# Evening out the slots of a fused FFT and GEGLU kernel, and two-pass values for five blocks in six

## The chip, the cores and the metric

The kernel runs on one core of a Trainium2 chip. The metric is device time in microseconds (us), the median of several runs. All runs quoted here are in the same (fast) state, with a granted TensorE clock of 0.994 to 1.0. PE is TensorE (PEld its weight loads), DVE is VectorE, ACT is ScalarE and POOL is GpSimd. PSUM is the memory that matmuls write to, in banks; copying a result out of a bank is called an *eviction* here.

## The reference, cut to what matters

```python
X = np.fft.fft(np.fft.fft(x, axis=1), axis=2).real      # x: 8 batches x 3008 x 256
g   = X @ w_gate                                        # 256 -> 1536
val = X @ w_val
out = (gelu(g) * val) @ w_out                           # 1536 -> 256
```

The kernel does the FFT as matmuls ("DFT work"). It uses the symmetry of a real input's transform: a token k and its mirror have the same even part E and odd part O, so gate and value are needed at E + O and at E − O.

## The kernel before

A batch has 3 chunks of 512, 512 and 481 token pairs, and a chunk has 12 blocks (`fc`) of 128 of the 1536 hidden columns. One turn of the loop over blocks is a *slot*. The weights "O" and "M" are the odd part and −2 times it, so a pass with M on top of E + O gives E − O in the same PSUM bank.

In the traces below, a matmul that starts a new result waits until the last reader of its bank is done. The kernel uses eight PSUM banks (2 + 3 + 1 + 2), and hands them out by tag:

```python
ps_g   bufs=2    # gate           ps_o   bufs=1    # layer-2 output
ps_v   bufs=3    # value          ps_dft bufs=2    # DFT
```

First half of a block, and second half (one slot later):

```python
def apart(ci, fc):
    return fc % 3 != 2 and (b, ci) != (0, 0)            # two blocks of three

def l1_first(ci, fc):
    pg = ps_g()
    mm(pg, "g", "E", E); mm(pg, "g", "O", O)            # (cut: slices, flags)
    activation(gl[:, 0], pg, Gelu)                      # ACT, first gelu
    pv = ps_v()
    if apart(ci, fc):                                   # value in two passes
        mm(pv, "v", "E", E)
        po = ps_v()
        mm(po, "v", "M", O)
        ve = EB * w128 + pv                             # DVE: three operations
        vv[:, 0]        = -0.5 * po + ve
        vv[:, reversed] =  0.5 * po + ve
    else:                                               # value in three passes
        mm(pv, "v", "E", E); mm(pv, "v", "O", O)
        h[:, fc, 0] = gl[:, 0] * pv                     # DVE

def l1_second(ci, fc):
    mm(pg, "g", "M", O)
    if apart(ci, fc):
        activation(gl[:, reversed], pg, Gelu)           # ACT, second gelu
        h[:, fc] = gl * vv                              # POOL, both halves
    else:
        mm(pv, "v", "M", O)
        activation(gl[:, 1], pg, Gelu)
        h[:, fc, reversed] = gl[:, 1] * pv              # DVE
```

Layer 2 of a chunk runs in the next chunk's slots, in 8 units of 12 matmuls each. *Filler* is DFT work of the next batch, spread over the slots. A slot was:

```python
for fc in range(NFC):                                   # NFC = 12
    first[fc]()
    ... DFT filler of the next batch ...
    if fc > 0: second[fc - 1]()
    tgt = len(pend) * (fc + 1) // NFC                   # 0 1 2 2 3 4 4 5 6 6 7 8
    while done < tgt: pend[done](); done += 1           # a unit: 12 matmuls
```

So two slots of three had 12 layer-2 matmuls and the third had none. The order in the program is not quite the order on the engine: the build moves some instructions ahead.

## Time and profile before

| | before |
|---|---|
| time | 719.29 us (median of 4 runs beside the changed kernel, 718.97 to 719.59) |
| busy: PE, DVE, ACT, POOL | 96%, 80%, 65%, 58% |
| value blocks in two / three passes | 184 / 104 |
| period of one batch in the steady state | 84.9 us |

These lines are from the page of the kernel before: the engines' busy time, the chain of waits by engine, and three groups of instructions (line, engine, operation, output and inputs, count, then busy us and mean ns of one, then the idle time of the engine before them and what ended most of it).

```profile
PE 688.0 (96%) x5274; PEld 460.5 (64%) x5336; DVE 572.3 (80%) x923; ACT 466.9 (65%) x892; POOL 412.2 (58%) x242
...
PE 88%; ACT 5%; DVE 4%; issue 2%; DMA 1%; POOL 0%; ACTq 0%; DVEq 0%
...
L551 POOL TENSOR_TENSOR h_sb<-gelu_sb,v_sb 128x1024 bf16<-128x1024 bf16 (+1 forms) x184 | 387.1, 2105 | 277.2 <-ACT gelu_sb L550 156.8
...
L524 DVE SCALAR_TENSOR_TENSOR ve_sb<-EB_sb,w_97,ps_v 128x512 f32<-128x512 bf16 (+1 forms) x184 | 134.1, 733 | 66.2 <-PE ps_v L502 66.0
...
L550 ACT ACTIVATE gelu_sb<-ps_g 128x512 bf16<-128x512 f32 (+1 forms) x184 | 108.6, 590 | 19.2 <-PE ps_g L502 17.7
```

PE is the engine to look at, but its busy share can't tell how much there is to gain. The Trainium skill says so in "Perfetto Trace Analysis", section "Identifying the Most-Contended Engine": matmul busy share is not a good measure of the distance from the roofline. What can be counted is the distance between the starts of two matmuls. For bf16 it is 216 ns for 512 columns, 203 for 481 and 109 for 256 when nothing is in the way. I call what a distance has beyond that a *gap*, and put it down to the PSUM tag that the late matmul writes.

The timeline of the kernel before, in a slot without layer 2, shows two such gaps. Its columns are start and duration in us, engine, line, operation, output and inputs, shapes and count.

```profile
325.84 0.38 PE L502 MATMUL ps_v<-EO_sb,WvE 128*128 128x512 bf16 x1
...
326.06 0.38 PE L502 MATMUL ps_v<-EO_sb,WvM 128*128 128x512 bf16 x1
...
326.26 0.75 DVE L524 SCALAR_TENSOR_TENSOR ve_sb<-EB_sb,w_97,ps_v 128x512 f32<-128x512 bf16 x1 [1.08 <-PE ps_v L502]
...
326.50 0.38 PE L502 MATMUL ps_g<-EO_sb,WgM 128*128 128x512 bf16 x1
...
326.72 0.38 PE L502 MATMUL ps_v<-EO_sb,WvM 128*128 128x512 bf16 x1
...
327.06 0.38 PE L502 MATMUL ps_v<-EO_sb,WvE 128*128 128x512 bf16 x1
...
327.20 0.59 ACT L554 ACTIVATE gelu_sb<-ps_g 128x512 bf16<-128x512 f32 x1
...
327.50 0.38 PE L502 MATMUL ps_g<-EO_sb,WgM 128*128 128x512 bf16 x1
...
327.84 0.38 PE L502 MATMUL ps_g<-EO_sb,WgE 128*128 128x512 bf16 x1
```

The value matmul at 327.06 comes 0.34 us after the matmul before it, not 0.216. It needs a value bank, and the DVE operation that reads one (326.26, 0.75 us long) ended at 327.01. The gate matmul at 327.84 again comes 0.34 us after its predecessor. The second gelu that frees a gate bank ran from 327.20 to 327.79.

### The profile page before, as it was taken

Reading aid. Unit: us, or ns where it says so; the run is one execution under the profiler, and the core shown is the slowest. Engines: PE = TensorE matmul, PEld = TensorE weight load, DVE = VectorE, ACT = ScalarE, POOL = GpSimd, SP = SyncE. Lnnn points to the kernel's source line nnn. Section 1 sums busy time; section 2 is a strip of 40 time slices with the busy share of each in tenths; the row PEclk is TensorE's granted clock in tenths of the full one; section 3 lists DMA queues with packets and bytes.
Section 4 is the critical chain, followed back from the end, with each engine's and each line's share of the span. In section 5 each row is a group of like instructions: output and inputs, shape, how many; then the busy total and the mean of one; then the engine's idle time right before and its main releaser. Section 6 shows DMA issues by size and latency. Waiting matters only on the chain.

```text
span 716.7 us, 14298 instructions
## 1 busy us (share of the span) xinstructions
PE 688.0 (96%) x5274; PEld 460.5 (64%) x5336; DVE 572.3 (80%) x923; ACT 466.9 (65%) x892; POOL 412.2 (58%) x242
## 2 busy tenths in 40 slices
PE   2899999999999999999999999999999999999995
PEld 2556666666667666666666666666666766666664
DVE  7698888798877888788877888779887788888870
ACT  6688567766676666766677656776668666666650
POOL 8205565655556565666566656555565656576760
PEclk9999999999999999999999999999999999999999
DMA  9951512431115111151212421111111111211122
GB/s 247 205 118 23 124 31 46 86 72 35 41 38 119 42 34 43 33 121 38 45 31 53 105 45 34 43 36 37 35 41 42 30 44 31 45 41 38 42 45 66
DMA packets 36277, 43.43 MB, mean 61 GB/s; under 512 B 6668, under 2 KB 33292, under 8 KB 34700
## 3 DMA queue, kind: packets, MB, share of 16 engines
q1 hardware_dynamic: 32432, 30.47, 17.8%
q0 software_dynamic: 3184, 11.57, 8.8%
q8 instruction: 41, 0.67, 0.4%
q10 hardware_dynamic: 592, 0.49, 0.3%
q14 instruction: 28, 0.23, 0.1%
HBM read 29.43 MB, written 24.64 MB: 75 GB/s over the span
## 4 chain that ended last, share of the span: by engine, by line
PE 88%; ACT 5%; DVE 4%; issue 2%; DMA 1%; POOL 0%; ACTq 0%; DVEq 0%
PE ps_o L573 33%; PE ps_g L502 23%; PE ps_v L502 20%; PE ps_dft L402 6%; PE ps_dft L365 3%; ACT gelu_sb L517 1%; ACT gelu_sb L554 1%; ACT A_sb L379 1%; PE ps_dft L427 1%; PE ps_dft L440 1%; DVE x_sb L236 1%; ACT out_sb L591 1%; DVE EO_sb L456 1%; PE ps_dft L452 1%; DVE h_sb L536 1%
## 5 line engine op out<-in xcount | busy, mean ns | idle before, releaser
L551 POOL TENSOR_TENSOR h_sb<-gelu_sb,v_sb 128x1024 bf16<-128x1024 bf16 (+1 forms) x184 | 387.1, 2105 | 277.2 <-ACT gelu_sb L550 156.8
L573 PE MATMUL ps_o<-Wo_sb,h_sb 128*128 128x256 bf16 (+1 forms) x2304 | 295.5, 272 | 4.0 <-DVE out_sb L584 2.2
L573 PEld LDWEIGHTS <-h_sb 128*128 128x128 bf16 (+1 forms) x2304 | 227.7, 100 | 68.3 <-issue 9.4
L517 ACT ACTIVATE gelu_sb<-ps_g 128x512 bf16<-128x512 f32 (+1 forms) x288 | 169.8, 590 | 123.2 <-PE ps_g L502 115.2
L524 DVE SCALAR_TENSOR_TENSOR ve_sb<-EB_sb,w_97,ps_v 128x512 f32<-128x512 bf16 (+1 forms) x184 | 134.1, 733 | 66.2 <-PE ps_v L502 66.0
L528 DVE SCALAR_TENSOR_TENSOR v_sb<-ps_v,ve_sb 128x512 f32<-128x512 f32 (+1 forms) x184 | 124.4, 676 | 13.9 <-POOL h_sb L551 0.5
L530 DVE SCALAR_TENSOR_TENSOR v_sb<-ps_v,ve_sb 128x512 f32<-128x512 f32 (+1 forms) x184 | 123.3, 670 | 0.0
L550 ACT ACTIVATE gelu_sb<-ps_g 128x512 bf16<-128x512 f32 (+1 forms) x184 | 108.6, 590 | 19.2 <-PE ps_g L502 17.7
L502 PE MATMUL ps_v<-EO_sb,WvE 128*128 128x512 bf16 (+1 forms) x288 | 107.8, 374 | 3.2
L502 PE MATMUL ps_g<-EO_sb,WgE 128*128 128x512 bf16 (+1 forms) x287 | 107.4, 374 | 1.6
L502 PE MATMUL ps_v<-EO_sb,WvM 128*128 128x512 bf16 (+1 forms) x288 | 108.0, 375 | 0.3 <-DVE v_sb L530 0.2
L502 PE MATMUL ps_g<-EO_sb,WgM 128*128 128x512 bf16 (+1 forms) x287 | 107.9, 376 | 0.1
L555 DVE TENSOR_TENSOR h_sb<-gelu_sb,ps_v 128x512 bf16<-128x512 bf16 (+1 forms) x104 | 69.7, 671 | 32.5 <-ACT gelu_sb L554 32.5
L591 ACT ACTIVATE out_sb<-ps_o 128x512 f32<-128x512 f32 x92 | 54.8, 595 | 51.2 <-PE ps_o L573 51.2
L502 PE MATMUL ps_g<-EO_sb,WgO 128*128 128x512 bf16 (+1 forms) x231 | 86.4, 374 | 0.0
L536 DVE TENSOR_TENSOR h_sb<-gelu_sb,ps_v 128x512 bf16<-128x512 bf16 (+1 forms) x104 | 69.9, 673 | 5.2 <-ACT gelu_sb L517 4.0
L554 ACT ACTIVATE gelu_sb<-ps_g 128x512 bf16<-128x512 f32 (+1 forms) x104 | 61.0, 590 | 6.3 <-PE ps_g L502 6.2
L412 DVE CAST Z_sb<-ps_dft 128x512 bf16<-128x512 f32 x88 | 60.1, 684 | 1.3 <-PE ps_dft L402 1.3
L402 PE MATMUL ps_dft<-CS,A_sb 128*128 128x256 bf16 x372 | 60.8, 274 | 0.4 <-DVE EO_sb L456 0.3
L402 PEld LDWEIGHTS <-A_sb 128*128 128x128 bf16 x384 | 37.8, 99 | 28.9 <-issue 1.8
L365 PEld LDWEIGHTS <-x_sb 94*128 94x128 bf16 x512 | 31.9, 102 | 31.3 <-DVE x_sb L236 14.9
L379 ACT ACTIVATE A_sb<-ps_dft 128x384 bf16<-128x384 f32 x115 | 50.9, 496 | 0.3 <-PE ps_dft L365 0.3
(102 smaller groups left out, 433.2 us busy)
## 6 DMA issues: line engine op xcount, KB each, us to landing
out_dram<-out_sb SPq DMA_DIRECT2D x361, 64.0 KB, 2.0
x_sb<-in_x_dram POOLq DMA_DIRECT2D x14, 752.0 KB, 8.1
x_plain<-in_x_dram SPq DMA_DIRECT2D x4, 384.0 KB, 7.6
x_plain<-in_x_dram SPq DMA_DIRECT2D x2, 768.0 KB, 7.6
Wo_sb<-in_moe_w_out_dram POOLq DMA_DIRECT2D x2, 384.0 KB, 5.8
wg_hi<-in_moe_w_gate_dram SPq DMA_DIRECT2D x2, 256.0 KB, 3.8
wv_hi<-in_moe_w_val_dram SPq DMA_DIRECT2D x2, 256.0 KB
wg_lo<-in_moe_w_gate_dram SPq DMA_DIRECT2D x2, 256.0 KB, 4.4
```

The costliest lines, as they stand in the source:

```text
L402: nc.tensor.matmul(ps[:, d * C : (d + 1) * C], A[:, cc, k2 + d, :], CS[:, cc, :], start=(cc == 0), stop=(cc == 1),)
L502: nc.tensor.matmul(ps[:, :n], W[nm, part][:, fs], src, start=start, stop=stop, **kw)
L517: nc.scalar.activation(gl[:, 0, :n], pg[:, :n], AF.Gelu)
L524: nc.vector.scalar_tensor_tensor(ve[:, :n], EB_bufs[b][:, c0 : c0 + n], w128[:, fc : fc + 1], pv[:, :n], op0=ALU.mult, op1=ALU.add)
L528: nc.vector.scalar_tensor_tensor(vv[:, 0, :n], po[:, :n], -0.5, ve[:, :n], op0=ALU.mult, op1=ALU.add)
L530: nc.vector.scalar_tensor_tensor(_sub(vv, [[-1, n]], TOK + n - 1), po[:, :n], 0.5, ve[:, :n], op0=ALU.mult, op1=ALU.add)
L536: nc.vector.tensor_tensor(st["h"][:, fc, 0, :n], gl[:, 0, :n], pv[:, :n], op=ALU.mult)
L550: nc.scalar.activation(_sub(gl, [[-1, n]], TOK + n - 1), pg[:, :n], AF.Gelu)
L551: nc.gpsimd.tensor_tensor(st["h"][:, fc, :, :n], gl[:, :, :n], pv[:, :, :n], op=ALU.mult)
L554: nc.scalar.activation(gl[:, 1, :n], pg[:, :n], AF.Gelu)
L555: nc.vector.tensor_tensor(_sub(st["h"], [[-1, n]], (fc * 2 + 1) * TOK + n - 1), gl[:, 1, :n], pv[:, :n], op=ALU.mult)
L573: nc.tensor.matmul(pso[:m, sign, :], st["h"][:, fc, sign, h0 : h0 + m], Wo_sb[:, fc, :], start=(fc == 0), stop=(fc == NFC - 1),)
```

## The change

Its intent: spread the work that DVE, ACT and POOL must do behind PE evenly over the slots, so that more blocks can use the two-pass value, which has one matmul less. Layer 2 comes in pieces of 4 matmuls, two per slot. The second gate pass moves from behind the filler to right behind the next block's first gate pass. Five blocks of six are in two passes.

```diff
         def apart(ci, fc):
-            return fc % 3 != 2 and (b, ci) != (0, 0)
+            return fc % 6 != 5 and (b, ci) != (0, 0)
 ...     # l1_first and l1_second are each split into a gate and a value half:
 ...     # l1_gate (G), l1_value (V), l1_gate2 (g), l1_value2 (v)
+        L2P = 4
-                for fc in range(NFC):
+                for fc in range(f0, f0 + L2P):
                     nc.tensor.matmul(pso[:m, sign, :], ...)
 ...
+    SLOT = "GgVvfLL"
 ...
-            for fc in range(NFC):
-                first[fc]()
-                ... filler ...
-                if fc > 0:
-                    second[fc - 1]()
-                tgt = len(pend) * (fc + 1) // NFC
-                while done < tgt: ...
+            for fc in range(NFC + 1):
+                for step in SLOT:
+                    if step in "GV" and fc < NFC:
+                        parts[step][fc]()
+                    elif step in "gv" and fc > 0:
+                        parts[step][fc - 1]()
+                    elif step == "L" and done < len(pend) and fc < NFC:
+                        pend[done]()
+                        done += 1
+                    elif step == "f" and fc < NFC:
+                        ... filler ...
```

More of the change, by code (lines that the diff above doesn't have):

```diff
@@ L498, in apart, with l1_gate @@
         def apart(ci, fc):
-            return fc % 3 != 2 and (b, ci) != (0, 0)
+            return fc % 6 != 5 and (b, ci) != (0, 0)
         def mm(ps, n, nm, part, fs, src, start, stop, **kw):
             nc.tensor.matmul(ps[:, :n], W[nm, part][:, fs], src, start=start, stop=stop, **kw)
-        def l1_first(ci, fc):
+        def l1_gate(ci, fc):
             def run():
@@ L517, in run, with l1_value @@
                 nc.scalar.activation(gl[:, 0, :n], pg[:, :n], AF.Gelu)
+                st["ps"][fc] = [pg, gl, None]
+            return run
+        def l1_value(ci, fc):
+            def run():
+                n = chunk_len[ci]
+                c0 = chunk_off[ci]
+                E, O = (EO_bufs[b][:, i, c0 : c0 + n] for i in range(2))
+                st = cstate[ci]
+                fs = slice(fc * 128, (fc + 1) * 128)
+                gl = st["ps"][fc][1]
                 pv = ps_v()
@@ L531, in run @@
                         _sub(vv, [[-1, n]], TOK + n - 1), po[:, :n], 0.5, ve[:, :n], op0=ALU.mult, op1=ALU.add)
-                    st["ps"][fc] = (pg, vv, gl)
+                    st["ps"][fc][2] = vv
                 else:
@@ L536, in run, with l1_gate2, l1_value2 @@
                     nc.vector.tensor_tensor(st["h"][:, fc, 0, :n], gl[:, 0, :n], pv[:, :n], op=ALU.mult)
-                    st["ps"][fc] = (pg, pv, gl)
+                    st["ps"][fc][2] = pv
             return run
-        def l1_second(ci, fc):
+        def l1_gate2(ci, fc):
+            def run():
+                n = chunk_len[ci]
+                c0 = chunk_off[ci]
+                O = EO_bufs[b][:, 1, c0 : c0 + n]
+                fs = slice(fc * 128, (fc + 1) * 128)
+                pg, gl, _ = cstate[ci]["ps"][fc]
+                mm(pg, n, "g", "M", fs, O, False, True, skip_group_check=True)
+                dst = _sub(gl, [[-1, n]], TOK + n - 1) if apart(ci, fc) else gl[:, 1, :n]
+                nc.scalar.activation(dst, pg[:, :n], AF.Gelu)
+            return run
+        def l1_value2(ci, fc):
             def run():
@@ L546, in run @@
                 fs = slice(fc * 128, (fc + 1) * 128)
-                pg, pv, gl = st["ps"].pop(fc)
-                mm(pg, n, "g", "M", fs, O, False, True, skip_group_check=True)
+                _, gl, pv = st["ps"].pop(fc)
                 if apart(ci, fc):
-                    nc.scalar.activation(_sub(gl, [[-1, n]], TOK + n - 1), pg[:, :n], AF.Gelu)
                     nc.gpsimd.tensor_tensor(st["h"][:, fc, :, :n], gl[:, :, :n], pv[:, :, :n], op=ALU.mult)
@@ L553, in run @@
                     mm(pv, n, "v", "M", fs, O, False, True, skip_group_check=True)
-                    nc.scalar.activation(gl[:, 1, :n], pg[:, :n], AF.Gelu)
                     nc.vector.tensor_tensor(
@@ L561, in last, with l2_piece @@
             return b == B - 1 and ci == len(groups) - 1
-        def l2_unit(ci, sub, sign):
+        L2P = 4
+        def l2_piece(ci, sub, sign, f0):
             def run():
@@ L568, in run @@
                 h0 = n - sub * 128 - m if sign else sub * 128
-                if sign == 0:
+                if (sign, f0) == (0, 0):
                     st["pso"][sub] = ps_o()
                 pso = st["pso"][sub]
-                for fc in range(NFC):
+                for fc in range(f0, f0 + L2P):
                     nc.tensor.matmul(
@@ L579, in run @@
                     )
+                if f0 + L2P < NFC:
+                    return
                 if last(ci):
@@ L598, in ffn_work @@
             nsub = (chunk_len[ci] + 127) // 128
-            first = [l1_first(ci, fc) for fc in range(NFC)]
-            second = [l1_second(ci, fc) for fc in range(NFC)]
+            parts = {k: [f(ci, fc) for fc in range(NFC)] for k, f in (
+                ("G", l1_gate), ("V", l1_value), ("g", l1_gate2), ("v", l1_value2))}
             subs = [nsub - 1, *range(nsub - 1)] if last(ci) else range(nsub)
-            l2s = [l2_unit(ci, s, g) for s in subs for g in range(2)]
-            chunks.append((first, second, l2s))
+            l2s = [l2_piece(ci, s, g, f) for s in subs for g in range(2) for f in range(0, NFC, L2P)]
+            chunks.append((parts, l2s))
         return chunks
+    SLOT = "GgVvfLL"
     head, s1_mm, s1_ev = dft_work(0)
@@ L679 @@
         fi = 0
-        for first, second, l2s in chunks:
+        for parts, l2s in chunks:
             done = 0
-            for fc in range(NFC):
-                first[fc]()
-                if b == 0 and slot < NFC:
-                    for _ in range(2):
-                        if early:
-                            early.pop(0)()
-                    for f in folds.get(slot, []):
-                        f()
-                tgt = max(0, len(filler) * (slot + 1 - first_slot) // (nslot - first_slot))
-                while fi < tgt:
-                    filler[fi]()
-                    fi += 1
-                if fc > 0:
-                    second[fc - 1]()
-                tgt = len(pend) * (fc + 1) // NFC
-                while done < tgt:
-                    pend[done]()
-                    done += 1
-                slot += 1
-            second[NFC - 1]()
+            for fc in range(NFC + 1):
[8 more added lines that the diff above has]
+                    elif step == "f" and fc < NFC:
+                        if b == 0 and slot < NFC:
+                            for _ in range(2):
+                                if early:
+                                    early.pop(0)()
+                            for f in folds.get(slot, []):
+                                f()
+                        tgt = max(0, len(filler) * (slot + 1 - first_slot) // (nslot - first_slot))
+                        while fi < tgt:
+                            filler[fi]()
+                            fi += 1
+                slot += fc < NFC
+            assert done == len(pend)
             pend = l2s
```

## The prediction

> **What bounds the kernel.** TensorE. The page gives PE 96% busy, DVE 80%, ACT 65%, POOL 58%; the chain of waits is 88% PE. Because matmul ends are modelled, I use start times in the timeline: 512-column matmuls follow each other every 216 ns, 481-column ones every 203, layer-2 ones (256 columns) every 109. The Trainium skill, "TensorE: Matmul & The Clock Gate", section "Wait — 56ns, not 53.3ns?", gives 215.7 ns for N = 512 at full clock; this trace agrees. Six of eight batches repeat with a period of 84.9 us. Matmul starts account for 82.3 us of it; 2.6 us are PE gaps (about 20 of 50 to 250 ns), so PE is 97% dense. A head of about 30 us and a tail of about 20 us (layer 2 of the last chunk, 2.0 us per 12 matmuls, one output PSUM buffer) don't change.
>
> **Removed.** Two-pass value blocks go from 184 to 230 (276 x 5/6). Each of the 46 saves one value matmul: 31 x 216 + 15 x 203 = 9.7 us of PE, all on the critical path: 1.2 us per batch.
>
> **Moved.** The second gate pass comes right behind the next block's first one; layer 2 comes as two pieces of four per slot rather than twelve in two slots of three. By what ended just before each PE gap, about half of the gap time (1.3 of 2.6 us per batch) is the next gate matmul waiting for the second gelu to free one of two gate banks. The early pass gives that gelu the rest of the slot (about 1.5 us), so these should go.
>
> **Added.** The other gaps are value matmuls waiting for DVE to free one of three value banks. A two-pass block costs DVE 0.87 + 0.60 + 0.60 = 2.07 us start to start (the second operation waits for the first's result), a three-pass block 1.2: 46 x 0.87 = 40 us more, 80% to about 85%. In a run of five two-pass blocks DVE needs 2.07 us per slot, 2.4 with a Z copy; PE needs 5 x 0.216 + 8 x 0.109 = 1.95, 2.39 with a 4-matmul DFT pack. So inside runs DVE is about level with PE, and only the sixth block (1.2 against 2.17) lets it catch up. POOL gains 46 products of 2.1 us: 58% to about 72%, 2.08 us back to back against a 1.95 to 2.3 us slot. I expect value-bank gaps to grow from 1.2 to about 2 us per batch, most in the last batch, which has no DFT filler.
>
> **Sum.** -9.7 us of matmuls, -8 to -10 of gate gaps, +5 to +8 of value gaps, something lost in rearrangement: about -12.5 us, 707 us, 1.7% faster. Range 699 to 715. Chances: faster by over 2% (below 705.2) 0.36, within 2% 0.62, slower 0.02.
>
> **What would show each step.** Right: 58 three-pass blocks instead of 104 (as many value-O matmuls), 230 POOL products; batch period near 83.3 us; no PE gap before a first gate matmul that ends with a second gelu; remaining gaps before value matmuls, ended by DVE; DVE near 85%, POOL near 71%; durations of single operations unchanged. Wrong: gate gaps remaining, or DVE waiting for POOL to free v_sb for more than a few us in the wait list.
>
> **What would make it wrong.** The build orders instructions itself (the trace of before shows matmuls of two slots interleaved), so even slots may already be there in part, or come out otherwise. If DVE or POOL bounds the five-block runs, the time stays at 710 to 716; if value banks give no trouble, it falls to 700.

## More of the kernel before

(Up to 68 of about 5,300 matmul records are missing in a trace. The weight-load records are complete, so I filled the missing matmuls in from them.)

## The result, and the profile after

The changed kernel takes 690.62 us (690.12 to 691.25, 4 runs) against 719.29, a ratio of 0.9602 (95% interval 0.9585 to 0.9619). That is 28.7 us or 4.0% faster. The prediction was 707 us with a range of 699 to 715, so the result lies outside it. A ratio here is the mean time of one kernel's fast runs over that of the other's of the same rounds, so not quite the ratio of the medians that are quoted.

The same lines from the page of the changed kernel:

```profile
PE 664.8 (96%) x5290; PEld 455.7 (66%) x5290; DVE 603.0 (87%) x969; ACT 452.1 (66%) x892; POOL 507.0 (74%) x288
...
PE 93%; POOL 3%; DVE 1%; ACT 1%; issue 1%; POOLq 0%; DVEq 0%; ACTq 0%
...
L572 POOL TENSOR_TENSOR h_sb<-gelu_sb,v_sb 128x1024 bf16<-128x1024 bf16 (+1 forms) x230 | 481.4, 2107 | 155.0 <-ACT gelu_sb L560 66.3
...
L535 DVE SCALAR_TENSOR_TENSOR ve_sb<-EB_sb,w_97,ps_v 128x512 f32<-128x512 bf16 (+1 forms) x230 | 167.6, 729 | 22.6 <-PE ps_v L502 19.7
L560 ACT ACTIVATE gelu_sb<-ps_g 128x512 bf16<-128x512 f32 (+1 forms) x288 | 168.0, 584 | 2.8 <-PE ps_g L502 2.8
```

There are 230 two-pass blocks. DVE went to 87% and POOL to 74%, while the single operations kept their length (2105 and 2107 ns for the POOL product, 733 and 729 ns for the first DVE operation). So the work went where it was meant to. The surprise is in the idle column of the first DVE operation. DVE waited 66.2 us in all before it, and now waits 22.6 us, although PE is no longer held up by DVE either.

A slot of the changed kernel, from its timeline:

```profile
120.20 0.38 PE L502 MATMUL ps_g<-EO_sb,WgE 128*128 128x512 bf16 x1
...
120.63 0.38 PE L502 MATMUL ps_g<-EO_sb,WgM 128*128 128x512 bf16 x1
...
120.85 0.38 PE L502 MATMUL ps_v<-EO_sb,WvE 128*128 128x512 bf16 x1
...
120.89 0.60 ACT L517 ACTIVATE gelu_sb<-ps_g 128x512 bf16<-128x512 f32 x1 [0.45 <-PE ps_g L502]
121.06 0.38 PE L502 MATMUL ps_v<-EO_sb,WvM 128*128 128x512 bf16 x1
...
121.27 0.75 DVE L535 SCALAR_TENSOR_TENSOR ve_sb<-EB_sb,w_97,ps_v 128x512 f32<-128x512 bf16 x1
121.28 0.51 PE L365 MATMUL ps_dft<-G,x_sb 94*128 94x96 bf16 x8
121.39 0.59 ACT L560 ACTIVATE gelu_sb<-ps_g 128x512 bf16<-128x512 f32 x1
...
121.62 1.04 PE L595 MATMUL ps_o<-Wo_sb,h_sb 128*128 128x256 bf16 x8
121.86 0.88 ACT L379 ACTIVATE A_sb<-ps_dft 128x384 bf16<-128x384 f32 x2
...
122.50 0.38 PE L502 MATMUL ps_g<-EO_sb,WgE 128*128 128x512 bf16 x1
```

The second gelu (121.39) starts on the heels of the first one and ends at 121.98, ahead of the filler's two evictions (L379). The next gate matmul is at 122.50, just when the eight layer-2 matmuls are through (121.62 + 8 x 0.109 = 122.49). PE waits for nothing. The gaps of the two kernels, in us, over the whole run by the tag of the bank written:

| | gate | value | DFT | layer 2 | sum of gaps over 40 ns | sum of all gaps |
|---|---|---|---|---|---|---|
| before, whole run | 14.6 | 12.7 | 9.7 | 5.2 | 42.2 | 45.7 |
| after, whole run | 3.7 | 7.9 | 8.6 | 5.3 | 25.4 | 28.7 |
| before, from 60 us on | 10.2 | 6.7 | 1.9 | 5.2 | 24.0 | 25.3 |
| after, from 60 us on | 0.1 | 0.9 | 0.5 | 5.3 | 6.8 | 7.9 |

(The whole-run rows hold about 2.6 us that are no gaps: the 16 fp32 matmuls of the head are counted at bf16 distances, and follow each other every 429 ns for 512 columns, not 216. It is the same in both kernels, so differences are not touched.)

The gaps fell by 17.0 us (45.7 − 28.7). With 9.7 us of matmuls less that makes 26.7 of the 27.2 us between the two spans (716.7 and 689.5). Nearly all gaps of the middle of the run are gone; what is left is the head (20.8 us up to 60 us, the 2.6 us included) and the tail. The period of a batch is now 81.0 us.

### The profile page after: what moved, and what is told of

It is laid out like the page before. It is cut to its first block, busy times and chain, and to the rows that moved or that the text cites. A ratio compares the mean times of both kernels' runs of the same rounds, so it can differ in the third digit from the quotient of the medians.

```text
span 689.5 us, 14359 instructions
## 1 busy us (share of the span) xinstructions
PE 664.8 (96%) x5290; PEld 455.7 (66%) x5290; DVE 603.0 (87%) x969; ACT 452.1 (66%) x892; POOL 507.0 (74%) x288
## 4 chain that ended last, share of the span: by engine, by line
PE 93%; POOL 3%; DVE 1%; ACT 1%; issue 1%; POOLq 0%; DVEq 0%; ACTq 0%
PE ps_o L595 36%; PE ps_g L502 26%; PE ps_v L502 19%; PE ps_dft L402 6%; PE ps_dft L365 3%; POOL h_sb L572 1%; PE ps_dft L452 1%; PE ps_dft L427 1%; PE ps_dft L440 1%; PE ps_v L332 0%; PE ps_g L332 0%; POOLq L758 0%; DVE out_sb L608 0%; DVE A_sb L381 0%; PE ps_v L402 0%
## 5 line engine op out<-in xcount | busy, mean ns | idle before, releaser
L572 POOL TENSOR_TENSOR h_sb<-gelu_sb,v_sb 128x1024 bf16<-128x1024 bf16 (+1 forms) x230 | 481.4, 2107 | 155.0 <-ACT gelu_sb L560 66.3
L595 PE MATMUL ps_o<-Wo_sb,h_sb 128*128 128x256 bf16 (+1 forms) x2304 | 299.2, 272 | 3.9 <-DVE out_sb L608 2.2
L595 PEld LDWEIGHTS <-h_sb 128*128 128x128 bf16 (+1 forms) x2304 | 220.5, 100 | 44.2 <-issue 5.0
L535 DVE SCALAR_TENSOR_TENSOR ve_sb<-EB_sb,w_97,ps_v 128x512 f32<-128x512 bf16 (+1 forms) x230 | 167.6, 729 | 22.6 <-PE ps_v L502 19.7
L539 DVE SCALAR_TENSOR_TENSOR v_sb<-ps_v,ve_sb 128x512 f32<-128x512 f32 (+1 forms) x230 | 155.4, 675 | 16.5 <-POOL h_sb L572 0.6
L541 DVE SCALAR_TENSOR_TENSOR v_sb<-ps_v,ve_sb 128x512 f32<-128x512 f32 (+1 forms) x230 | 153.8, 669 | 0.0
L502 PE MATMUL ps_g<-EO_sb,WgO 128*128 128x512 bf16 (+1 forms) x288 | 108.2, 376 | 0.0
L402 PE MATMUL ps_dft<-CS,A_sb 128*128 128x256 bf16 x372 | 56.8, 274 | 0.3 <-DVE EO_sb L456 0.3
L575 DVE TENSOR_TENSOR h_sb<-gelu_sb,ps_v 128x512 bf16<-128x512 bf16 (+1 forms) x58 | 39.2, 677 | 15.0 <-ACT gelu_sb L560 13.0
L379 ACT ACTIVATE A_sb<-ps_dft 128x384 bf16<-128x384 f32 x115 | 50.9, 503 | 0.6 <-PE ps_dft L365 0.5
L502 PEld LDWEIGHTS <-WvE 128*128 128x128 bf16 x288 | 28.2, 98 | 32.2
L502 PEld LDWEIGHTS <-WvM 128*128 128x128 bf16 x288 | 28.2, 98 | 30.8 <-issue 0.8
```

The source lines that it names most:

```text
L402: nc.tensor.matmul(ps[:, d * C : (d + 1) * C], A[:, cc, k2 + d, :], CS[:, cc, :], start=(cc == 0), stop=(cc == 1),)
L502: nc.tensor.matmul(ps[:, :n], W[nm, part][:, fs], src, start=start, stop=stop, **kw)
L535: nc.vector.scalar_tensor_tensor(ve[:, :n], EB_bufs[b][:, c0 : c0 + n], w128[:, fc : fc + 1], pv[:, :n], op0=ALU.mult, op1=ALU.add)
L539: nc.vector.scalar_tensor_tensor(vv[:, 0, :n], po[:, :n], -0.5, ve[:, :n], op0=ALU.mult, op1=ALU.add)
L541: nc.vector.scalar_tensor_tensor(_sub(vv, [[-1, n]], TOK + n - 1), po[:, :n], 0.5, ve[:, :n], op0=ALU.mult, op1=ALU.add)
L572: nc.gpsimd.tensor_tensor(st["h"][:, fc, :, :n], gl[:, :, :n], pv[:, :, :n], op=ALU.mult)
```

## The experiments

The theory after the result (A): PE is the bound. The steady gaps come from uneven slots, in which the same tag is asked for again too soon. Even slots take nearly all of them away whatever the ratio of blocks, and the ratio is worth its matmuls and no more. Rival B: the three-pass blocks make the value gaps, since each of them holds a value bank until its second gelu, so that the new ratio alone is the cure. The prediction itself is a third view: more DVE work makes value gaps grow.

All times and gaps are collected here. The gaps are us in the stretch from 120 to 600 us of each run, counting those over 40 ns.

| run | time us | gate | value | DFT | layer 2 |
|---|---|---|---|---|---|
| before | 719.5 | 7.9 | 5.6 | 1.5 | 0 |
| after | 690.6 | 0.1 | 0 | 0 | 0 |
| even_old_ratio | 700.4 | 0.1 | 0 | 0 | 0 |
| five_in_six_old_slots | 715.9 | 10.6 | 4.7 | 3.7 | 0 |
| late_gate_pass | 712.0 | 17.6 | 0.6 | 0 | 0 |
| lumpy_layer2 | 708.3 | 12.0 | 1.8 | 0 | 0 |
| gate_before_filler | 692.8 | 0 | 0 | 0.4 | 0 |
| late_gate_three_banks | 705.9 | 0 | 0.6 | 10.4 | 0 |
| two_value_banks | 705.8 | 0.5 | 10.1 | 0 | 0 |
| all_two_pass | 703.2 | 0.4 | 0.5 | 1.1 | 8.1 |
| tail_banks | 686.1 | 0.1 | 0 | 0 | 0 |
| eleven_in_twelve | 683.4 | 0.7 | 0 | 0 | 0 |
| eleven_in_twelve_but_last | 683.1 | 0.7 | 0 | 0 | 0 |

### Even slots, old ratio

```diff
 # against the changed kernel
-            return fc % 6 != 5 and (b, ci) != (0, 0)
+            return fc % 3 != 2 and (b, ci) != (0, 0)
```

> The changed kernel with two of three blocks in two value passes, as before. Theory A (nearly all PE gaps come from uneven slots; the ratio only removes 46 value matmuls): steady PE gaps fall from 2.6 to below 0.3 us per batch, time 690.6 + 9.7 = about 700 us. Rival B (the fewer three-pass blocks, each of which holds a value bank until its second gelu, are what removes the value-bank gaps): value-bank gaps of about 1.2 us per batch stay, about 709 us.

Measured: 700.44 us (699.69 to 700.74), 0.9737 of before (0.9722 to 0.9751). The steady gaps are 0.1 us. So even slots alone are worth 19.1 us, and the ratio on top of them 9.8 us (700.44 − 690.62), which is its 46 matmuls. Rival B falls: with all of the 104 three-pass blocks in place there are no value gaps. (Even slots here means both halves of the change, even layer 2 and the early second gate pass; the square below takes them apart.)

### The ratio alone, in the old slots

```diff
 # against the kernel before
-            return fc % 3 != 2 and (b, ci) != (0, 0)
+            return fc % 6 != 5 and (b, ci) != (0, 0)
```

> The kernel before with only the ratio changed to five in six. Theory A: saves 9.7 us of matmuls but value-bank gaps grow as DVE gets 40 us more work in uneven slots: 710 to 716 us. Rival B: 9.7 us of matmuls and about 9 us of value-bank gaps saved, 700 us.

Measured: 715.86 us (715.77 to 716.01), 0.9953 of before (0.9938 to 0.9968). Of the 9.7 us of matmuls only 3.7 us arrive. The time is in the range of theory A, but the way there is not what I had written: value gaps did not grow (5.6 to 4.7 us). Gate gaps grew (7.9 to 10.6) and DFT gaps too (1.5 to 3.7). A saved matmul makes a slot shorter, so the gate bank is asked for sooner while the second gelu needs as long as before. That is a reading of the gaps; no run tests it apart.

### Late second gate pass, and layer 2 in lumps

```diff
 # late_gate_pass, against the changed kernel
-    SLOT = "GgVvfLL"
+    SLOT = "GVfgvLL"
```

> The changed kernel with the second gate pass back behind the value and the DFT filler (slot order gate, value, filler, second gate, second value, two layer-2 pieces). Theory A with the early pass as the cure of gate-bank gaps: gate gaps return to about 1.3 us per batch, about 700 us. If even layer-2 pieces alone give the second gelu enough time (0.87 us of layer 2 between it and the next gate matmul): about 691 us.

```diff
 # lumpy_layer2, against the changed kernel
-        L2P = 4
+        L2P = 12
-    SLOT = "GgVvfLL"
+    SLOT = "GgVvfL"
-                    elif step == "L" and done < len(pend) and fc < NFC:
-                        pend[done]()
-                        done += 1
+                    elif step == "L" and fc < NFC:
+                        while done < len(pend) * (fc + 1) // NFC:
+                            pend[done]()
+                            done += 1
```

> The changed kernel with layer 2 back in pieces of twelve in two slots of three, early gate pass and five in six kept. Theory A with even layer 2 as the cure of value-bank gaps: DVE gets 2.07 us of work in slots of 1.1 us plus filler, then 2.4 us; gaps of 2 us per batch or more in front of value matmuls, 704 us or more. If the early gate pass is the whole cure: about 691 us.

Measured: late_gate_pass 712.03 us (711.51 to 712.29), lumpy_layer2 708.32 us (707.81 to 708.73). The loss of late_gate_pass is larger than expected (about 700). The time of lumpy_layer2 lies in the expected range (704 or more), but the reason given for it was wrong: 2 us or more of value gaps per batch were expected, and there are 1.8 us in six batches, against 12.0 us of gate gaps. With five_in_six_old_slots and the changed kernel the two make a square, all at five blocks in six:

| | layer 2 in lumps | layer 2 even |
|---|---|---|
| second gate pass late | 715.9 | 712.0 |
| second gate pass early | 708.3 | 690.6 |

Alone, even layer 2 gains 3.8 us and the early gate pass 7.5. Together they gain 25.2. Each alone moves the wait elsewhere. Value gaps fall with either of them (4.7 to 0.6 or 1.8), which I had not expected of the gate pass; why it helps them stays open. Gate gaps grow with either (10.6 to 17.6 or 12.0) and vanish only with both. Of the 12.0 us with the early pass alone, 3.5 us (34 gaps) are of a new kind: it is a second pass that waits, for the first gelu of its own block.

The timeline of late_gate_pass shows why even layer 2 is not enough:

```profile
372.88 0.51 PE L365 MATMUL ps_dft<-G,x_sb 94*128 94x96 bf16 x8
...
373.22 0.38 PE L502 MATMUL ps_g<-EO_sb,WgM 128*128 128x512 bf16 x1
...
373.36 0.87 ACT L379 ACTIVATE A_sb<-ps_dft 128x384 bf16<-128x384 f32 x2
373.44 1.03 PE L595 MATMUL ps_o<-Wo_sb,h_sb 128*128 128x256 bf16 x8
374.10 0.62 ACT L560 ACTIVATE gelu_sb<-ps_g 128x512 bf16<-128x512 f32 x1
...
374.76 0.38 PE L502 MATMUL ps_g<-EO_sb,WgE 128*128 128x512 bf16 x1
```

The second gate matmul starts at 373.22, but its gelu waits until 374.10, because the two evictions of the filler's result (L379, 0.87 us) stand ahead of it in ACT's queue. Layer 2 (eight matmuls from 373.44) is through at 374.31. The next gate matmul comes at 374.76, 0.05 us after the gelu's end, with one value matmul pulled forward meanwhile. The whole stretch from 120 to 600 us looks like this: all 86 gate gaps end with a second gelu, and in 74 of them that gelu ran directly behind an eviction of the filler.

### Second gate pass behind the value but before the filler

```diff
-    SLOT = "GgVvfLL"
+    SLOT = "GVgvfLL"
```

> The changed kernel with the second gate pass behind the value matmuls but still ahead of the DFT filler (slot order gate, value, second gate, second value, filler, two layer-2 pieces). It splits what late_gate_pass changed. If late_gate_pass lost its 21 us because the filler's two evictions (0.87 us) stood ahead of the second gelu in ACT's queue: gate gaps near 0 and about 691 us. If it lost them because the pass came later on PE (0.43 us of value matmuls) and left the second gelu too little of the slot: gate gaps of several us in the stretch 120 to 600 us, 697 us or more.

Measured: 692.81 us (692.46 to 692.96), no gate gaps. So the pass need not come right behind the first one; it is enough that it, and with it the second gelu on ACT, comes before the filler. (This order also spares the pass the filler's own matmuls on PE, 0.34 us in the slot above. That ACT's queue is the larger part is read from the 74 of 86 gaps; no run moves the gelu alone.) Its timeline has the same five kinds of instruction in the new order:

```profile
371.38 0.38 PE L502 MATMUL ps_g<-EO_sb,WgM 128*128 128x512 bf16 x1
...
371.80 0.60 ACT L560 ACTIVATE gelu_sb<-ps_g 128x512 bf16<-128x512 f32 x1
...
371.94 1.04 PE L595 MATMUL ps_o<-Wo_sb,h_sb 128*128 128x256 bf16 x8
372.30 0.87 ACT L379 ACTIVATE A_sb<-ps_dft 128x384 bf16<-128x384 f32 x2
...
372.82 0.38 PE L502 MATMUL ps_g<-EO_sb,WgE 128*128 128x512 bf16 x1
```

The gelu ends at 372.40 and the next gate matmul is not late. The 0.43 us of value matmuls by which the pass is later than in the change cost 2.2 us of time at most; no gap over 40 ns explains them.

### Late second gate pass with a third gate bank

```diff
 # against late_gate_pass
-        ... tag="g", bufs=2 ...          # ps_g
+        ... tag="g", bufs=3 ...
-        ... tag="dft", bufs=2 ...        # ps_dft
+        ... tag="dft", bufs=1 ...
-            tag, n = (("dft", 2), ("g", 2), ("v", 3))[turn[0] % 3]
+            tag, n = (("g", 3), ("v", 3))[turn[0] % 2]
-                    ... _sub(st["ps_b"], [[1, n]], 0, part_num=1), AF.Copy)
+                    ... _sub(st["EB"], [[1, n]], chunk_off[gi], part_num=1), AF.Copy)
```

> late_gate_pass with three gate banks instead of two, paid for with one DFT bank instead of two (the one-row copy that needed two reads the same values from SBUF). If its gaps are waits for a gate bank (theory A): gaps in front of the first gate matmul fall from 15.7 us in the stretch 120 to 600 us to below 2 us; DFT matmuls get gaps of their own, about 0.5 us per first-stage pack, 4 us per batch or less; time 693 to 705 us. If the late second pass costs for another reason (order of ACT, POOL): gate gaps stay near 15 us, 712 us or more.

The last two lines of the diff let the one-row copy read from SBUF, since there is only one DFT bank. Measured: 705.94 us (705.56 to 706.66). Gate gaps fell from 17.6 to 0. (The expectation has 15.7 us, an earlier count.) So they were waits for a gate bank. DFT gaps of 10.4 us came in their place, 55 of about 0.2 us each, less than the 0.5 us that I had expected. The time is still 0.9 us beyond the expected range; the gaps of its head (the first 60 us) are 2.6 us more than those of late_gate_pass (22.7 and 20.1).

### Two value banks

```diff
-        return psum_pool.tile([128, 512], FP32, tag="v", bufs=3, name="ps_v")
+        return psum_pool.tile([128, 512], FP32, tag="v", bufs=2, name="ps_v")
-            tag, n = (("dft", 2), ("g", 2), ("v", 3))[turn[0] % 3]
+            tag, n = (("dft", 2), ("g", 2), ("v", 2))[turn[0] % 3]
```

> The changed kernel with two value banks instead of three. Theory A: the second value matmul of a block then waits until DVE has done all three operations of the block before (2.15 us plus its lag after that block's first value matmul, against 2.17 us from there to it), so value-bank gaps of 0.1 to 0.5 us in nearly every two-pass block: 715 to 760 us, gaps all in front of value matmuls. If DVE's lag were no matter: 691 us.

Measured: 705.84 us (705.65 to 706.1). The direction is right (value gaps 0 to 10.1 us), the size is not: there are 76 gaps of about 0.13 us in the stretch, well under one per two-pass block, and the time is below the range. So the third bank holds DVE's lag back from PE. Even two banks do so for most blocks if the slots are even.

### Every block in two passes

```diff
-            return fc % 6 != 5 and (b, ci) != (0, 0)
+            return (b, ci) != (0, 0)
```

> The changed kernel with every block (but the first chunk's) in two value passes: 46 more value matmuls less, 9.7 us of PE. Theory A (PE bounds, DVE lags inside runs of five two-pass blocks and is brought back by the sixth, within the slack of the three value banks): without the sixth block nothing brings DVE back; DVE needs about 36 x 2.07 + 15 x 0.60 = 83 us per batch less what fills its dependency wait, against 79.7 us of PE, so DVE becomes the bound: 688 to 694 us, value-bank gaps appear. Rival C (DVE has real slack): 681 us and no gaps.

Measured: 703.17 us (702.07 to 703.38), 12.5 us slower than the change, and neither theory. Value gaps are 0.5 us in the stretch from 120 to 600 us at a DVE load of 94% (452.8 us in 480). That alone does not prove rival C's slack, since PE is held up by layer 2 there (8.1 us), which may give DVE time. eleven_in_twelve below is the clean case: DVE is busy for 449.4 us of 480, also 94%, with no value gap over 40 ns. What became the bound in all_two_pass is POOL, which neither had looked at. First the busy times in a stretch of 75 us of the last batch of all_two_pass (the stretch, its length, then busy us and count of PE, PEld, DVE, ACT and POOL, then granted clock, DMA share and GB/s):

```profile
600.00:675.00 75.00, 70.61 (x457) 44.81 (x461) 66.54 (x107) 43.98 (x84) 72.01 (x36) 1.00 0.19 43
```

The same view of the changed kernel, in a stretch that lies as far before its tail:

```profile
590.00:665.00 75.00, 74.78 (x522) 49.52 (x521) 68.20 (x109) 47.72 (x91) 64.36 (x32) 1.00 0.19 42
```

POOL's own timeline in the last batch of all_two_pass (start and duration of an unbroken row of products):

```profile
632.49 25.14 POOL L572 TENSOR_TENSOR h_sb<-gelu_sb,v_sb 128x1024 bf16<-128x1024 bf16 x12 [1.02 <-DVE v_sb L541]
658.65 21.87 POOL L572 TENSOR_TENSOR h_sb<-gelu_sb,v_sb 128x962 bf16<-128x962 bf16 x11 [1.02 <-DVE v_sb L541]
```

And from the view of the layer-2 line of all_two_pass, for what PE and its weight loads stood idle before it (us, times):

```profile
  POOL h_sb L572: 29.4, 43
```

POOL makes 12 products without a break in 25.1 us, 2.1 us each, while PE's slot is 5 x 0.216 + 8 x 0.109 = 1.95 us. Layer 2 waits for products. POOL is 96% busy in that stretch of all_two_pass (72.01 of 75), and 86% in that of the changed kernel (64.36 of 75). The Trainium skill comes close to this cost: "GPSIMD Engine Reference", section "3.1 Elementwise — side-by-side cycle accounting", gives 4497 ns for a two-input operation with N = 2048 in fp32, so an estimate of 2.25 us for 1024 (half of it), and the trace of the kernel before has 2.14 for a product of bf16 and fp32.

### The tail, and a ratio in between

```diff
 # tail_banks: layer 2 of the last chunk
-                if (sign, f0) == (0, 0):
-                    st["pso"][sub] = ps_o()
-                pso = st["pso"][sub]
+                if last(ci):
+                    if f0 == 0:
+                        st["pso"][sub, sign] = ps_v() if (2 * sub + sign) % 2 else ps_g()
+                    bank = st["pso"][sub, sign]
+                    pso = _sub(bank, [[0, 2], [1, C]], 0)
+                else:
+                    ... as before ...
```

> The changed kernel with the last chunk's layer 2 alternating over the gate and value banks, free by then, instead of one output bank. All theories: 7 waits of about 0.6 us in the tail go, 686 to 687 us.

Measured: 686.14 us (685.55 to 686.52), 4.5 us faster than the change, as expected. Two units of 12 matmuls in the tail of the changed kernel, with one bank, from the chain that ended last (start and duration in us, engine, tile, line, count):

```profile
674.00 1.49 PE ps_o L595 x12
675.98 1.48 PE ps_o L595 x12
```

And two units of tail_banks, from its timeline:

```profile
673.00 1.47 PE L601 MATMUL ps_v<-Wo_sb,h_sb 128*128 128x256 bf16 x12
674.31 1.47 PE L601 MATMUL ps_g<-Wo_sb,h_sb 128*128 128x256 bf16 x12
```

They follow each other every 1.98 us in the first and every 1.31 us, or 12 x 0.109, in the second.

```diff
 # eleven_in_twelve, against tail_banks
-            return fc % 6 != 5 and (b, ci) != (0, 0)
+            return fc % 12 != 11 and (b, ci) != (0, 0)
 # eleven_in_twelve_but_last
+            return fc % (6 if b == B - 1 else 12) != (5 if b == B - 1 else 11) and (b, ci) != (0, 0)
```

> tail_banks with eleven blocks of twelve in two value passes (23 value matmuls less, 4.9 us of PE). all_two_pass showed POOL as the next bound: with no three-pass block, layer 2 waited for products. If one three-pass block in twelve is enough for POOL (11 x 2.08 + 2 DMA issues against 26.5 us of PE per chunk with DFT, 23.6 without): about 681.5 us, few layer-2 gaps. If POOL still lags, above all in the last batch: 686 us or more, with layer-2 gaps that end with POOL products.

> tail_banks with eleven of twelve in the batches that have DFT filler and five of six in the last batch, which has none. If POOL has its slack from the filler's PE time: 682 us, without layer-2 gaps up to the tail, and at least as fast as eleven_in_twelve.

Measured: 683.40 us (682.63 to 683.58) and 683.06 us (682.42 to 683.45). Both beat tail_banks, the change and the kernel before (0.9499 and 0.9496 of it), and they can't be told apart from each other. One three-pass block in twelve is enough to keep POOL in step. (tail_banks ran on another chip; the kernel before took 719.56 us beside it and 719.18 beside these two, so 0.4 us of the gains may be that.) The times are a little above the expected 681.5 and 682. The first saves 23 matmuls and gains 2.7 us of 4.9; the second saves 20 and gains 3.1 us of about 4.2. The gaps from 120 to 600 us grew by 0.6 us in both, and from 600 us on the first has 1.3 us more of them than the second.

## Why the prediction was wrong

- **The bound, and the matmuls saved: right.** "-9.7 us of matmuls", all on the critical path. Measured 9.8 us as the difference between even_old_ratio and the change, in which no new gap eats it.
- **Gate gaps: right in size, half right in cause.** "-8 to -10 of gate gaps". From 60 us on they fell from 10.2 to 0.1 us. I put it down to the early pass alone, which "gives that gelu the rest of the slot". The square shows that the early pass alone leaves them at 12.0 us; it needs the even layer 2 to make the rest of the slot long enough. So the size came out right in part by luck. gate_before_filler shows what the early pass contributes: the second gelu gets ahead of the filler's evictions on ACT.
- **Value gaps: wrong, and this is the step that failed.** "I expect value-bank gaps to grow from 1.2 to about 2 us per batch", "+5 to +8 of value gaps". From 60 us on they fell from 6.7 to 0.9 us. The swing is 11 to 14 us of the 16.4 us by which the prediction was off. I had read in the trace that the value gaps end with DVE operations and concluded that DVE was too slow, so that more DVE work means more gaps. But DVE itself was waiting in the same run: 66 us for PE before its first operation of a block, as the group's idle column shows, and 32.5 us for ACT before the second product of a three-pass block (L555). An engine that is both late and idle in one run need not be too slow; here it was kept waiting and then hurried. The 45 value gaps from 120 to 600 us (5.6 us) can be followed back to DVE's last wait of over 0.2 us. In 27 of them (2.6 us) it had waited for PE's value matmul, in 17 (2.7 us) for the second gelu of a three-pass block, in one for POOL. The second kind looks like this in the timeline of the kernel before, with the DVE operations of the next block standing behind the product in DVE's queue:

```profile
142.59 0.69 DVE L555 TENSOR_TENSOR h_sb<-gelu_sb,ps_v 128x512 bf16<-128x512 bf16 x1 [1.53 <-ACT gelu_sb L554]
...
143.20 0.74 DVE L524 SCALAR_TENSOR_TENSOR ve_sb<-EB_sb,w_97,ps_v 128x512 f32<-128x512 bf16 x1
...
143.99 0.38 PE L502 MATMUL ps_v<-EO_sb,WvM 128*128 128x512 bf16 x1
```

  The value matmul that L524 reads started at 142.14; L524 starts at 143.20, behind L555, and its end at 143.94 lets the second value matmul of the block after that start (0.12 us late). As for the uneven feeding, the starts of the first value matmuls of two neighbouring blocks, between 120 and 600 us, are 1.18 to 3.73 us apart before, 68 of 204 distances under 1.8 us. After, they are 1.89 to 2.61 us apart. DVE needs 2.07 us for a two-pass block. Spacing alone is not the whole cause, though: lumpy_layer2 still has 62 of 206 distances under 1.8 us and only 1.8 us of value gaps, and all 12 of those follow a wait for a second gelu. That DVE's speed was not the cause is shown; how much the spacing and how much the late gelu contributed was not tested apart.
- **DVE level with PE inside a run of five two-pass blocks: right, but nearly harmless.** The last batch of the changed kernel has no filler, and there the lag can be read (PE's first value matmul of a block, then DVE's first operation on it):

```profile
600.08 0.38 PE L502 MATMUL ps_v<-EO_sb,WvE 128*128 128x512 bf16 x1
...
600.97 0.74 DVE L535 SCALAR_TENSOR_TENSOR ve_sb<-EB_sb,w_97,ps_v 128x512 f32<-128x512 bf16 x1
...
602.03 0.38 PE L502 MATMUL ps_v<-EO_sb,WvE 128*128 128x512 bf16 x1
...
603.05 0.73 DVE L535 SCALAR_TENSOR_TENSOR ve_sb<-EB_sb,w_97,ps_v 128x512 f32<-128x512 bf16 x1
...
603.99 0.38 PE L502 MATMUL ps_v<-EO_sb,WvE 128*128 128x512 bf16 x1
...
605.12 0.73 DVE L535 SCALAR_TENSOR_TENSOR ve_sb<-EB_sb,w_97,ps_v 128x512 f32<-128x512 bf16 x1
```

  The lag grows from 0.89 to 1.02 to 1.13 us, 0.12 per block, as 2.07 − 1.95 says. Five blocks make 0.6 us of it, and the three value banks nearly take that up: the last batch has three value gaps, 0.9 us in all, each at the last block of a chunk, where the second value pass waits for a product (L547) that stands behind DVE's backlog. That batch is where the prediction had looked for most of the value gaps. I had compared the two rates and forgotten to ask how much lag the banks allow. two_value_banks (10.1 us of gaps) and eleven_in_twelve (none from 120 to 600 us, at the same three banks) show that the slack is in the banks, and that with three of them DVE is not what bounds, even at 94%.
- **DFT gaps: left out.** They fell too (1.9 to 0.5 us from 60 us on), 1.4 us that my sum did not have.
- **Other marks of the profile.** 58 three-pass blocks and 230 products: right. DVE 87% (predicted 85), POOL 74% (71 to 72), unchanged durations: right. Batch period 81.0 us against 83.3: wrong, for the reason above.
- **"even slots may already be there in part":** they were not. The build does pull single matmuls forward, but at the same ratio the even slots are worth 19.1 us (before and even_old_ratio).

The Trainium skill says in "Perfetto Trace Analysis", section "Optimization Strategy", that the same gap repeating on the engine that should be saturated can mean that there isn't enough SBUF or PSUM for the next tile. The gaps here repeated from batch to batch, and they were waits for banks (late_gate_three_banks: 17.6 us to 0). But the cure in the change added no bank. It gave each bank's reader the time between two uses.

## What to carry to other kernels

When the bounding engine shows many short waits for an engine that is itself often idle, look at the spacing of the requests, and at what its queue is stuck behind, before blaming its load: even spacing and the order in the in-order queue of the reader can take the waits away while the load goes up. Changes of order are worth testing as a square, since here two of them gained 3.8 and 7.5 us alone and 25.2 together. Before pushing work onto the next engine, compare its time per slot with the slot *and* with what the buffers let it lag, and do it for every engine in the chain: here DVE had room and POOL was the one that ran out.

## What the Trainium skill lacked or had wrong

- "VectorE: DVE Perf Modes", section "The DRAIN you can't avoid", says, from eight copies with and without a semaphore after each, that the semaphore costs nothing extra. That can't be carried over to an operation that waits for the result of the one just before it. Start to start, the first operation of a two-pass block to the second, which reads its result, took 869 ns (median of 122 pairs in the changed kernel). With a Z copy (DVE's eviction of a DFT result) put between them, the first to the copy took 655 ns and the copy to the second 601. A dependent successor costs about 0.2 us more.
- I found no page that says how much a reader of PSUM may lag before TensorE waits, as a function of banks and slot. Here, in the last batch, a lag that grew by 0.6 us over five blocks made three gaps (0.9 us) with three value banks. From 120 to 600 us, three banks made none and two banks made 10.1 us.
- "Perfetto Trace Analysis", section "Optimization Strategy", tells to find the gaps between slices on the engine in question. For PE's matmuls that shows too little, because their slices overlap: in the kernel before, PE is idle for 28.7 us (716.7 − 688.0), while the distances between starts hold 45.7 us of gaps (2.6 of them the fp32 matmuls). From 120 to 600 us it is 476.0 us busy of 480, with gaps over 40 ns of 15.0 us. I found no page that tells to count gaps by starts, though the page that the prediction cites gives the distance between starts.
